# One weight load per page of instructions, a second bank for ranks, and a matmul block moved ahead of the last ranks

## The chip, the core and the metric

The kernel runs on one core of a Trainium2 chip. A core has five engines with a queue each: TensorE (PE, matrix products and transposes; PEld is its load of stationary weights), VectorE (DVE), ScalarE (ACT), GpSimd (POOL) and SyncE (SP), which here mostly starts DMA transfers. Every queue is served in order. Sixteen DMA engines move data between HBM and SBUF, and also bring the engines their instructions. PE writes only into PSUM, which has eight banks of 512 float32 per partition. The metric is the device time of one launch in microseconds; lower is better.

## The reference

Linear attention feeds a mixture of experts with one expert per token, and its output goes through a gated feed-forward layer.

```python
def phi(x):                                   # q, k: (2, 8, 576, 64), w_phi: (64, 128)
    proj = einsum('bhsd,df->bhsf', x, w_phi)
    proj = proj - max(abs(proj), axis=-1)
    return concatenate([exp(proj), exp(-proj)], axis=-1)
kv = einsum('bhsf,bhsd->bhfd', phi(k), v);  z = sum(phi(k), axis=2)
x  = (phi(q) @ kv) / (phi(q) @ z + 1e-6)      # as 1152 tokens of 512
e  = argmax(x @ w_gate);  g = softmax(x @ w_gate)[e]      # 8 experts
pos = number of earlier tokens with the same expert       # the token's rank
y  = g * (relu(x @ w1[e]) @ w2[e]) if pos < capacity else 0
out = (silu(y @ w_gate2) * (y @ w_val)) @ w_out           # 512 -> 1536 -> 512
```

## The kernel before

The 1152 tokens are nine tiles of 128. A first loop over tiles makes the k side (features, then the sums kv and z). A second loop over tiles, `for t in range(NT)` at line 664, makes the q side. It is a pipeline written out by hand: while tile t is projected and its exponentials are made, `q_num` (line 443) multiplies tile t-1 with kv in two halves of heads, `q_norm` divides tile t-2, `q_first` chooses its expert, and `q_rank` and `q_place` (lines 501 and 509) find the rank of each token of tile t-3 among those of its expert. After the loop the last tiles run out of the pipeline (lines 889 to 926).

`bank[6]` and `bank[7]` take the numerators of even tiles, `bank[2]` and `bank[3]` those of odd tiles. `sm` is another name for `bank[7]`, and all ranks are written there, into columns beyond the numerators. The second half of heads of an even tile therefore goes into the bank from which `q_place` has just to read the ranks of an earlier even tile, and PE holds that step back until VectorE has read them.

The tokens of a chosen expert are gathered by index (`gather`, GpSimd), transposed by PE (`transpose_x`), and go through the expert's two weight matrices in eight blocks. `h_mm(f)` is a block of the first matrix (eight matmul passes over 288 tokens), `y_mm(f)` the same block of the second. The expert with most tokens in the first tiles is the first item. Its weights, `raw[0]` to `raw[3]`, come in eight halves of 512 KB each: `h_mm(0)` and `h_mm(1)` read the first half of `raw[0]`, `h_mm(4)` and `h_mm(5)` the first of `raw[2]`. A second and a third item follow, then the feed-forward layer, whose weights arrive as `m2w` and are unpacked by ScalarE and VectorE beside the items.

`Paced` (line 79) counts the instructions that PE is given, and at every 256 of them, a page, lets transfers begin behind that step. Transfers in its list `waiting` come first; what is left of a page's budget, in KB, goes to the list `spare`, where the eight halves are put at tile 4. The budget is `FULL` = 800, and for tile 6 `MUCH` = 2048. `T.more(n)` starts n spare transfers at once, with no PE step to wait for.

Of the kernel before, what the change touches and what calls it, by code (L numbers as in the profile page):

```python
# [14 lines left out]
ALU = mybir.AluOpType  # L15
# [12 lines left out]
NT = N // P  # L28
E = 8
# [5 lines left out]
T0 = 2  # L35
# [9 lines left out]

MID = [(0, 0), (0, 1), (1, 0), (1, 1), (6, 0), (6, 1), (2, 0), (2, 1), (3, 0), (3, 1), (7, 0), (7, 1)]

PAGE, FIRST, ROOM, FULL, MUCH = 256, 193, 1060, 800, 2048

BESIDE = {  # L50
    0: {3: (("conv",),), 4: (("conv",),), 5: (("conv",),), 6: (("conv",),), 7: (("conv",),), 8: (("conv",),)},
# [18 lines left out]
RANK = [320] * (NT - 1) + [352]  # L70
# [8 lines left out]
class Paced:  # L79

    def __init__(self, engine):
        self.engine, self.count, self.at, self.waiting, self.spare, self.full = engine, 2, FIRST, [], iter(()), FULL

    def matmul(self, out, lhsT, rhs, **kw):
        return self.step(self.engine.matmul(out, lhsT=lhsT, rhs=rhs, **kw), 4 if lhsT.dtype == F32 else 2)  # L85
# [11 lines left out]
    def begin(self, x):  # L97

        used = 0
        while self.waiting and used + self.waiting[0][0] <= ROOM:  # L100
            size, load = self.waiting.pop(0)
            load(x)
            used += size
        while not self.waiting and used < self.full and self.count > FIRST + PAGE:
            size, load = next(self.spare, (self.full, None))
            if load is not None and used + size > self.full:
                self.spare = chain([(size, load)], self.spare)
                break
            if load is not None:
                load(x)  # L110
            used += size
# [13 lines left out]
def build(tc, qT, kT, v, wblk, wg, wexp, m2w, cap, cst, ids, out):  # L125
    nc = tc.nc
    ctx = ExitStack()
    V, A, G, T = nc.vector, nc.scalar, nc.gpsimd, Paced(nc.tensor)

    with ctx, tc.manual_schedule():  # L130
# [13 lines left out]
        capf = p0.tile([P, 1], F32, name="capf")  # L144
        sc = p0.tile([P, 4, 2, 12], F32, name="scan")
        est = p0.tile([P, 4, E], F32, name="est")
# [12 lines left out]
        ohsum = p0.tile([P, E], BF16, name="ohsum")  # L159
# [12 lines left out]
        bank = [pair[:, 0:512], pair[:, 512:1024], *(psm.tile([P, 512], F32, name=f"bank{j}") for j in range(2, 8))]  # L172
        xt, sm = bank[6:8]
# [6 lines left out]
        onebf = warm[:, 0:P]  # L180
# [13 lines left out]
        def behind(x, i):  # L194

            if i is not None:
                tc.add_manual_dep(x.ins, i.ins.name, mybir.DependencyInfo(mybir.DependencyClass.Sync, mybir.DependencyReason.DATA),
                                  reason="a load begins behind this step")
# [92 lines left out]
        def load_half(e, c, a, step=None):  # L291

            cols = slice(a * 1024, a * 1024 + 1024)
            behind(nc.sync.dma_start(out=raw[c][:, cols], in_=wexp[ds(e, 1), c].rearrange("a p f -> p (a f)")[:, cols]), step)
# [33 lines left out]
        if True:  # L328
# [4 lines left out]
            st = {}  # L333
# [38 lines left out]
            def later(size, load, *arg):  # L372
                T.later(size, lambda step: load(*arg, step))
# [5 lines left out]
            def g_turn(s, bk):  # L379

                for hp in range(NP):
                    T.transpose(bk[:, hp * P : hp * P + P], kvt[:, s, hp * P : hp * P + P], ident)
# [110 lines left out]
            def q_gate(t):  # L493
# [4 lines left out]
                A.activation(ex, lg, AF.Exp, scale=-1.0, bias=mx[:, 0:1], accum_out=mx[:, 2:3])  # L498
                A.activation(st[t + 1]["den"][:, H : H + 1], mx[:, 2:3], AF.Copy, bias=1e-9)

            def q_rank(t, *ahead):

                for c, w in ((RANK[t], ubf), *(((384, onebf),) if t in (T0 - 1, T0, NT - 1) else ())):
                    T.matmul(sm[:, c : c + E], lhsT=w, rhs=st[t]["oh"][2], start=True, stop=False)
                    for a in ahead:
                        T.matmul(sm[:, c : c + E], lhsT=onebf, rhs=st[a]["oh"][2], start=False, stop=False)
                    T.matmul(sm[:, c : c + E], lhsT=onebf, rhs=ohsum, start=False, stop=True)

            def q_place(t):

                mx, oh, ohb, lg = st[t]["oh"]
                V.tensor_tensor_reduce(oh, sm[:, RANK[t] : RANK[t] + E], ohb, 1.0, 0.0, ALU.mult, ALU.add, mx[:, 3:4])
                if t < NT - 2:
                    V.tensor_tensor(ohsum, ohsum, ohb, ALU.add)
                if t == T0 - 1:
                    V.tensor_copy(cnt0, sm[:, 384 : 384 + E])

            def q_put(t):

# [82 lines left out]
            def first_count():  # L602

                V.tensor_scalar(est[:, 0], cs[:, C_R8 : C_R8 + E], e0f[:, 1:2], None, ALU.is_equal)
                V.scalar_tensor_tensor(cnt0, sm[:, 384 : 384 + E], capf, est[:, 0], ALU.min, ALU.mult)

            def first_rest():

# [50 lines left out]
            cnt0 = pa.tile([P, E], F32, name="cnt0", bufs=1)  # L659
# [3 lines left out]
            for t in range(NT):  # L663
                if t + 3 < NT:
                    later(256, x_load, NT + t + 3)
                st[t + 1] = {}
                T.full = MUCH if t == T0 + 4 else FULL
                if t == 1:
                    g_turn(0, bank[2])
                    g_turn(1, bank[3])  # L670
                st[t]["pm"] = pb.tile([P, H, FP], F32, name="pm")
                maxima = less_max(bP, st[t]["pm"])
                norm = q_norm(t - 2) if t > 1 else iter(())
                late_ops = st[t - 3]["ops"] if t > 2 else iter(())
                next(maxima)
                next(maxima)
                next(late_ops, None)
                next(norm, None)
                next(late_ops, None)
                if t == 0:  # L680
                    k_sum(8, 9)
                else:
                    q_num(t - 1, 0)
                if t > 1:
                    q_phi(t, 0)
                if t > 2:
                    q_rank(t - 3)
                next(maxima)
                next(norm, None)
                if t > 2:  # L690
                    q_place(t - 3)
                if t == T0 + 3:
                    first_count()
                next(maxima)
                if t == 0:
                    k_take(1)
                    g_pack(1)
                    xrow = slot([96, 3, DM], F32, "xrow")
                    G.memset(xrow, 0.0)
                if t == 1:  # L700
                    g_copy(0, bank[2])
                    g_copy(1, bank[3])
                if t < 2:
                    q_phi(t, 0)
                step = q_exp(t, 0)
                if t == T0 + 5:
                    gather(0, (0, 1), step)
                elif t > 2:
                    q_put(t - 3)
                if t > 2:  # L710
                    x_store(t - 3, st[t - 2]["den"][:, H : H + 1])
                next(norm, None)
                if t:
                    q_num(t - 1, 1)
                if t == 1:
                    g_cols(1, bank[2])
                if t > 1:
                    ops = st[t - 2]["ops"] = q_first(t - 2)
                    choice = first_expert() if t == 4 else iter(())
                    for _ in range(3):  # L720
                        next(ops)
                        next(choice, None)
                    next(choice, None)
                    q_gate(t - 2)
                if t + 1 < NT:
                    T.until(lambda: NT + t + 1 in xraw)
                    project(xraw.pop(NT + t + 1), bP)
                q_phi(t, 1)
                step = q_exp(t, 1)
                if t == T0 + 5:  # L730
                    gather(0, (2,), step)
                    q_put(t - 3)
                if t == 4:
                    xch = slot([P, 4, 96, 3], F32, "xch")
                    raw = [slot([P, 2048], F32, f"raw{j}") for j in range(NC1)]
                    e = expert_of(0)
                    halves = [(512, lambda step, n=n: load_half(e, n // 2, n % 2, step)) for n in range(8)]
                    T.spare = chain(halves, T.spare)
                if t == T0 + 3:
                    load_list(0)  # L740
# [9 lines left out]
        def h_mm(f):  # L750
            c, r = f // 2, f % 2
            hp = bank[4 + f % 2][:, 0:WIN]
            for k in range(4):
                T.matmul(hp, lhsT=raw[c][:, k * 256 + r * P : k * 256 + r * P + P], rhs=xch[:, k].rearrange("p a b -> p (a b)"),
                         start=(k == 0), stop=(k == 3))
            A.activation(hh[f % 2], hp, AF.Relu)
# [129 lines left out]
        t = NT - 1  # L886
        def finish(ops):
            for _ in ops:
                pass
# [27 lines left out]
        h_mm(0)  # L917
        q_gate(t)
        finish(ops)
        q_rank(t - 1)  # L920
        q_rank(t, t - 1)
        for i in (t - 1, t):
# [3 lines left out]
        last = st[t + 1]["den"][:, H : H + 1]  # L926
        V.reciprocal(last, last)
        x_store(t, last)
        T.more(1)
        h_mm(1)  # L930
        y_mm(0)
        h_mm(2)
        y_mm(1)
# [3 lines left out]
        e = expert_of(1)  # L937
# [229 lines left out]
```

## Time and profile before

| | us |
|---|---|
| median of 3 runs (298.84 to 300.84) | 299.86 |
| the profiled execution | 297.08 |
| its span | 295.2 |
| PE busy in it | 280.4 (95%) |
| DVE, ACT, POOL busy in it | 193.8, 132.0, 41.4 |

The span runs from the first instruction to the last of the profiled execution. The times in the rows further down are microseconds from the span's start. A row of a timeline gives start, duration, engine, line, operation, what it writes and reads, and how many equal instructions in a row it stands for; in brackets is how long the engine stood idle before it, and what released it. Busy times of engines overlap. Only the idle time of an engine that the others wait for costs anything.

### The profile page before, as it was taken

How to read it: one execution, taken by the hardware profiler on the slowest of the kernel's cores; microseconds unless marked ns; L12 is line 12 of the kernel's file. 1: busy time of each engine (PE TensorE's matmuls, PEld its weight loads, DVE VectorE, ACT ScalarE, POOL GpSimd, SP SyncE). 2: the span in 40 equal slices, each digit the busy share in tenths (PEclk: the TensorE clock that was granted, in tenths of full speed). 3: DMA queues.
4: the chain of work that ended last, by engine and by line, in shares of the span. 5: the costliest groups of instructions: out<-in, count | busy, mean ns of one | idle time of the engine just before them, and what ended most of it. 6: DMA issues, size and time to landing. Idle time of an engine off the chain costs nothing. (4 is left out here: it accounts for less than half of the span.)

```text
span 295.2 us, 7725 instructions
## 1 busy us (share of the span) xinstructions
PE 280.4 (95%) x3195; PEld 243.3 (82%) x3195; DVE 193.8 (66%) x402; ACT 132.0 (45%) x255; POOL 41.4 (14%) x65
## 2 busy tenths in 40 slices
PE   7999999989979999999999999999999999999990
PEld 5899988877867777877775999999999899999970
DVE  1996885999948386799954788879876433223320
ACT  2877554767663242546456643553423322211210
POOL 3001030352654220006000000000010040000011
PEclk9999999999979999999999999999999999999998
DMA  6577654557973499999599205000416020000002
GB/s 210 180 233 205 194 183 156 168 203 210 321 260 116 126 322 381 417 405 359 194 394 363 91 2 143 0 2 0 142 52 271 2 109 0 0 2 1 2 2 75
DMA packets 18238, 47.96 MB, mean 162 GB/s; under 512 B 4353, under 2 KB 5542, under 8 KB 15632
## 3 DMA queue, kind: packets, MB, share of 16 engines
q1 hardware_dynamic: 16064, 44.39, 42.8%
q0 software_dynamic: 1264, 2.57, 2.6%
q8 instruction: 27, 0.44, 0.6%
q10 hardware_dynamic: 864, 0.39, 0.5%
q14 instruction: 19, 0.16, 0.2%
HBM read 41.06 MB, written 6.87 MB: 162 GB/s over the span
## 5 line engine op out<-in xcount | busy, mean ns | idle before, releaser
L85 PE MATMUL bank<-yh,m2h 128*128 128x384 f32 (+1 forms) x192 | 35.3, 305 | 0.0
L85 PE MATMUL bank<-yh,m2l 128*128 128x384 f32 (+1 forms) x192 | 35.2, 305 | 0.0
L85 PE MATMUL bank<-yl,m2h 128*128 128x384 f32 (+1 forms) x192 | 35.2, 305 | 0.0
L85 PE MATMUL bank<-xch,raw 128*128 128x288 f32 x128 | 33.7, 407 | 0.0
L85 PEld LDWEIGHTS bank<-yh,m2h 128*128 128x128 f32 x192 | 30.4, 188 | 2.5 <-issue 0.8
L995 ACT ACTIVATE th<-bank 128x384 fp32r<-128x384 f32 (+1 forms) x24 | 10.3, 431 | 43.2 <-DVE bank L994 43.2
L85 PEld LDWEIGHTS bank<-xch,raw 128*128 128x128 f32 x128 | 24.2, 190 | 6.6
L85 PEld LDWEIGHTS bank<-yh,m2l 128*128 128x128 f32 x192 | 29.6, 189 | 0.0
L85 PEld LDWEIGHTS bank<-yl,m2h 128*128 128x128 f32 x192 | 29.5, 189 | 0.0
L992 DVE TENSOR_TENSOR sg<-bank,sg 128x384 f32<-128x384 f32 (+1 forms) x24 | 11.6, 482 | 24.4 <-ACT sg L991 24.4
L85 PE MATMUL bank<-yk,phq 128*64 128x73 f32 x576 | 23.6, 235 | 2.5 <-issue 0.9
L85 PEld LDWEIGHTS bank<-yk,phq 128*64 128x64 f32 x576 | 20.8, 141 | 4.0 <-issue 1.4
L347 DVE TENSOR_REDUCE m<-bank 128x4 f32<-128x512 f32 x26 | 17.8, 686 | 8.4 <-PE bank L85 8.3
L283 DVE TENSOR_TENSOR m2l<-m2x,m2h 128x1024 fp32r<-128x1024 f32 x18 | 21.3, 1222 | 2.8 <-ACT m2h L282 2.7
L438 ACT ACTIVATE phq<-pair 128x512 f32<-128x512 f32 x36 | 19.5, 592 | 7.7 <-PE pair L88 7.6
L85 PE MATMUL bank<-vau,ph 128*64 128x65 f32 x640 | 21.9, 224 | 0.7 <-ACT ph L406 0.6
L85 PEld LDWEIGHTS bank<-vau,ph 128*64 128x64 f32 x640 | 20.1, 137 | 2.8 <-ACT ph L406 1.9
L991 ACT ACTIVATE sg<-bank 128x384 f32<-128x384 f32 (+1 forms) x24 | 10.3, 431 | 22.7 <-PE bank L85 22.7
L232 DVE SCALAR_TENSOR_TENSOR m2x<-es_mid,m2x 128x1024 uint32<-128x1024 uint32 x12 | 14.7, 1226 | 8.5 <-ACT es_mid L229 7.3
L996 DVE TENSOR_TENSOR tl<-bank,th 128x384 fp32r<-128x384 f32 (+1 forms) x24 | 11.6, 483 | 12.7 <-ACT th L995 12.7
L85 PE MATMUL bank<-m2h,th 128*128 128x512 f32 x48 | 19.1, 398 | 0.0
L85 PE MATMUL bank<-m2h,tl 128*128 128x512 f32 x48 | 19.1, 397 | 0.0
(159 smaller groups left out, 494.8 us busy)
## 6 DMA issues: line engine op xcount, KB each, us to landing
raw<-wexp SPq DMA_DIRECT2D x8, 1024.0 KB, 7.5
r<-m2w SPq DMA_DIRECT2D x8, 1024.0 KB, 8.0
r<-m2w SPq DMA_DIRECT2D x24, 256.0 KB, 4.0
raw<-wexp SPq DMA_DIRECT2D x8, 512.0 KB, 5.0
r_mid<-m2w SPq DMA_DIRECT2D x4, 1024.0 KB, 9.5
vau<-v SPq DMA_DIRECT2D x10, 260.0 KB, 3.6
qkr<-kT SPq DMA_DIRECT2D x9, 256.0 KB, 3.3
qkr<-qT SPq DMA_DIRECT2D x9, 256.0 KB, 2.8
```

The costliest lines, as they stand in the source:

```text
L85: return self.step(self.engine.matmul(out, lhsT=lhsT, rhs=rhs, **kw), 4 if lhsT.dtype == F32 else 2)
L232: V.scalar_tensor_tensor(w, es.bitcast(U32), 3, w, ALU.logical_shift_left, ALU.bitwise_or)
L283: V.tensor_tensor(m2l[j][:, sl], x[:, sl], m2h[j][:, sl], ALU.subtract)
L347: V.tensor_reduce(m[:, gs], pv, AX.X, ALU.max, apply_absolute_value=True)
L438: x = A.activation(st[t]["phq"][:, s, :, gs], bF[:, :, gs], AF.Exp, scale=1.0 - 2 * s)
L991: A.activation(s, pg, AF.Sigmoid)
L992: V.tensor_tensor(s, pg, s, ALU.mult)
L995: A.activation(th[f % 3][:, n], pv, AF.Copy)
L996: V.tensor_tensor(tl[f % 3][:, n], pv, th[f % 3][:, n], ALU.subtract)
```

## The change

The page budget stays at 800 KB throughout, so that one half (512 KB) begins per page and never four; the rest is started by `T.more(4)` behind the store of the last tile, where one half was started before. The ranks of tiles 0, 2, 4 and 6 go to `bank[3]`, the others stay in `bank[7]`. `h_mm(1)` stands ahead of the ranks of tiles 7 and 8, and no longer behind them and all that is made of them.

```diff
-PAGE, FIRST, ROOM, FULL, MUCH = 256, 193, 1060, 800, 2048
+PAGE, FIRST, ROOM, FULL = 256, 193, 1060, 800
...
-        while not self.waiting and used < self.full and self.count > FIRST + PAGE:
-            size, load = next(self.spare, (self.full, None))
-            if load is not None and used + size > self.full:
+        while not self.waiting and used < FULL and self.count > FIRST + PAGE:
+            size, load = next(self.spare, (FULL, None))
+            if load is not None and used + size > FULL:
...
+            ranks = [bank[3] if t % 2 == 0 and t < NT - 1 else sm for t in range(NT)]
+
             def q_rank(t, *ahead):
                 for c, w in ((RANK[t], ubf), *(((384, onebf),) if t in (T0 - 1, T0, NT - 1) else ())):
-                    T.matmul(sm[:, c : c + E], lhsT=w, rhs=st[t]["oh"][2], start=True, stop=False)
+                    r = ranks[t][:, c : c + E]
+                    T.matmul(r, lhsT=w, rhs=st[t]["oh"][2], start=True, stop=False)
...
-                V.tensor_tensor_reduce(oh, sm[:, RANK[t] : RANK[t] + E], ohb, 1.0, 0.0, ALU.mult, ALU.add, mx[:, 3:4])
+                V.tensor_tensor_reduce(oh, ranks[t][:, RANK[t] : RANK[t] + E], ohb, 1.0, 0.0, ALU.mult, ALU.add, mx[:, 3:4])
...
-                T.full = MUCH if t == T0 + 4 else FULL
...
         q_gate(t)
         finish(ops)
+        h_mm(1)
         q_rank(t - 1)
         q_rank(t, t - 1)
...
         x_store(t, last)
-        T.more(1)
-        h_mm(1)
+        T.more(4)
         y_mm(0)
```

How this moves instructions is seen at three places. The first is the queue of SP where the halves of the first item's weights begin (`raw_1304` to `raw_1307` are `raw[0]` to `raw[3]`, `xd<-yk` the stores of finished tiles). Lines with - stand there in the kernel before, with + in the changed one.

```order
 L294 DMA raw_1304<-wexp 128x1024
+L473 DMA xd<-yk 128x512
 L294 ISA
 L294 DMA raw_1305<-wexp 128x1024
+L473 DMA xd<-yk 128x512
 L294 ISA
 L294 DMA raw_1305<-wexp 128x1024
+L473 DMA xd<-yk 128x512 x3
 L294 ISA
 L294 DMA raw_1306<-wexp 128x1024
-L473 DMA xd<-yk 128x512
```

Two stores now stand between the second, third and fourth half, and all three last stores ahead of the other four halves, which follow each other.

The second place is PE in the second loop, tile 7: the ranks of tile 4 and then the second half of heads of tile 6 (`yk,phq`).

```order
 L85 LDWEIGHTS ubf_88
-L85 MATMUL bank7_102<-ohb_1514,ubf_88 128x8
+L85 MATMUL bank3_98<-ohb_1514,ubf_88 128x8
 L85 LDWEIGHTS warm_103
-L85 MATMUL bank7_102<-ohsum_87,warm_103 128x8
+L85 MATMUL bank3_98<-ohsum_87,warm_103 128x8
 L85 MATMUL bank7_102<-yk_92,phq_1481 64x73 x16
```

The ranks leave the bank into which the next sixteen matmuls write. The same holds for the ranks of tiles 0, 2 and 6.

The third place is PE where the pipeline runs out: the first item's block 0 (`xch,raw_1304` into `bank_99`), block 1 (into `bank_100`) and the ranks of tile 7.

```order
 L85 MATMUL bank_102<-yk,phq 64x73 x16
 L85 MATMUL bank_99<-xch,raw_1304 128x288 x4
+L85 MATMUL bank_100<-xch,raw_1304 128x288 x4
 L85 LDWEIGHTS ubf
 L85 MATMUL bank_102<-ohb,ubf 128x8
```

Block 1 moves ahead of the ranks; with the ranks, all that VectorE, GpSimd, ScalarE and SP make of them comes behind it.

## Rows read from the trace of the kernel before

**Rows 1.** The page, busy time and share of the span by engine.

```profile
PE 280.4 (95%) x3195; PEld 243.3 (82%) x3195; DVE 193.8 (66%) x402; ACT 132.0 (45%) x255; POOL 41.4 (14%) x65
```

**Rows 2.** Windows: length, busy time (instructions) by engine, granted clock, DMA share, GB/s.

```profile
71.40:80.90 9.50, 8.80 (x223) 7.71 (x220) 8.95 (x35) 6.62 (x17) 5.71 (x8) 1.00 0.95 298
84.00:87.70 3.70, 3.68 (x40) 3.12 (x40) 0.14 (x2) 2.40 (x6) 1.99 (x5) 0.54 0.54 202
92.70:153.00 60.30, 60.30 (x265) 47.10 (x263) 45.39 (x67) 25.59 (x38) 11.01 (x11) 1.00 0.85 314
```

**Rows 3.** Timeline of PE from tile 7 of the second loop to `y_mm(0)`.

```profile
74.00 1.25 PE L85 MATMUL bank<-yk,phq 128*64 128x73 f32 x32 [0.40 <-DVE mx L512]
...
81.85 0.60 PE L85 MATMUL bank<-yk,phq 128*64 128x73 f32 x11 [0.89 <-issue]
...
82.64 0.52 PE L88 MATMUL bank<-cs,xrow 96*128 96x96 f32 x4
84.02 0.80 PE L88 MATMUL bank<-cs,xrow 96*128 96x96 f32 x4 [0.86 <-DMA xrow<-xd,li]
...
85.62 2.15 PE L85 MATMUL bank<-yk,phq 128*64 128x73 f32 x32
87.71 2.21 PE L85 MATMUL bank<-xch,raw 128*128 128x288 f32 x8
...
90.51 0.17 PE L85 MATMUL bank<-ohb,ubf 128*128 128x8 bf16 x1 [0.57 <-DVE ohb L490]
...
90.67 2.19 PE L85 MATMUL bank<-xch,raw 128*128 128x288 f32 x8
92.69 1.13 PE L85 MATMUL pair<-hh,raw 128*128 128x288 f32 x4
```

**Rows 4.** Timeline of SP: where the first item's halves begin.

```profile
71.18 2.05 SPq L294 DMA_DIRECT2D raw<-wexp  x4
...
76.35 0.33 SPq L294 DMA_DIRECT2D raw<-wexp  x1
...
93.91 0.34 SPq L294 DMA_DIRECT2D raw<-wexp  x1
```

**Rows 5.** DMA queues, window 70.25 to 70.5: packets, MB, share of 16 engines.

```profile
q8 instruction: 1, 0.02, 23.0%
```

**Rows 6.** DMA queues, window 79.0 to 79.25: the next packet of that queue.

```profile
q8 instruction: 1, 0.02, 29.2%
```

**Rows 7.** DMA issues, window 66 to 92: count, median us from issue to landing.

```profile
xrow<-xd,li POOLq DMA_INDIRECT x3, 8.1
```

**Rows 8.** DMA issues, whole span: indirect stores at the kernel's end.

```profile
out<-room,gid POOLq DMA_INDIRECT x5, 2.9
```

**Rows 9.** Waits of PE up to 130 us: total us, times, longest.

```profile
PE bank L85 <- DVE cnt L605: 0.8, 1, 0.8
PE bank L85 <- DVE mx L512: 0.8, 2, 0.4
```

**Rows 10.** Timeline of DVE: tile 6's first maximum; tile 6's chosen expert.

```profile
66.78 0.69 DVE L347 TENSOR_REDUCE m<-bank 128x4 f32<-128x512 f32 x1 [0.21 <-PE bank L85]
...
81.31 0.22 DVE L490 TENSOR_SCALAR ohb<-oh,mx 128x8 bf16<-128x8 f32 x1
```

**Rows 11.** Timeline of ACT: last exponentials of the loop; a copy of transposed tokens.

```profile
81.36 1.06 ACT L438 ACTIVATE phq<-pair 128x512 f32<-128x512 f32 x2
...
85.73 0.69 ACT L321 ACTIVATE xch<-pair 128x384 f32<-128x384 f32 x1 [0.18 <-PE pair L88]
```

**Rows 12.** DMA issues, window 92 to 100: the eighth half alone.

```profile
raw<-wexp SPq DMA_DIRECT2D x1, 512.0 KB, 3.6
```

**Rows 13.** Tile `raw`, 60 to 180 us: landing times of all its loads.

```profile
DMA to landing us min/median/max: 3.6/6.7/13.6
```

**Rows 14.** Timeline of POOL: last gather of the second item.

```profile
104.54 0.95 POOL L309 DMA_INDIRECT xrow<-xd,li  x1 [0.31 <-PE bank L85]
```

**Rows 15.** Timeline of PE: transposes of the second item's tokens.

```profile
117.91 1.16 PE L88 MATMUL bank<-cs,xrow 96*128 96x96 f32 x12
```

More of the change, by code (lines that the diff above doesn't have):

```diff
@@ L81, in __init__ @@
     def __init__(self, engine):
-        self.engine, self.count, self.at, self.waiting, self.spare, self.full = engine, 2, FIRST, [], iter(()), FULL
+        self.engine, self.count, self.at, self.waiting, self.spare = engine, 2, FIRST, [], iter(())
     def matmul(self, out, lhsT, rhs, **kw):
@@ L499, in q_gate @@
                 A.activation(st[t + 1]["den"][:, H : H + 1], mx[:, 2:3], AF.Copy, bias=1e-9)
+            ranks = [bank[3] if t % 2 == 0 and t < NT - 1 else sm for t in range(NT)]
             def q_rank(t, *ahead):
                 for c, w in ((RANK[t], ubf), *(((384, onebf),) if t in (T0 - 1, T0, NT - 1) else ())):
-                    T.matmul(sm[:, c : c + E], lhsT=w, rhs=st[t]["oh"][2], start=True, stop=False)
+                    r = ranks[t][:, c : c + E]
+                    T.matmul(r, lhsT=w, rhs=st[t]["oh"][2], start=True, stop=False)
                     for a in ahead:
-                        T.matmul(sm[:, c : c + E], lhsT=onebf, rhs=st[a]["oh"][2], start=False, stop=False)
-                    T.matmul(sm[:, c : c + E], lhsT=onebf, rhs=ohsum, start=False, stop=True)
+                        T.matmul(r, lhsT=onebf, rhs=st[a]["oh"][2], start=False, stop=False)
+                    T.matmul(r, lhsT=onebf, rhs=ohsum, start=False, stop=True)
             def q_place(t):
                 mx, oh, ohb, lg = st[t]["oh"]
-                V.tensor_tensor_reduce(oh, sm[:, RANK[t] : RANK[t] + E], ohb, 1.0, 0.0, ALU.mult, ALU.add, mx[:, 3:4])
+                V.tensor_tensor_reduce(oh, ranks[t][:, RANK[t] : RANK[t] + E], ohb, 1.0, 0.0, ALU.mult, ALU.add, mx[:, 3:4])
                 if t < NT - 2:
@@ L515, in q_place @@
                 if t == T0 - 1:
-                    V.tensor_copy(cnt0, sm[:, 384 : 384 + E])
+                    V.tensor_copy(cnt0, ranks[t][:, 384 : 384 + E])
             def q_put(t):
@@ L604, in first_count @@
                 V.tensor_scalar(est[:, 0], cs[:, C_R8 : C_R8 + E], e0f[:, 1:2], None, ALU.is_equal)
-                V.scalar_tensor_tensor(cnt0, sm[:, 384 : 384 + E], capf, est[:, 0], ALU.min, ALU.mult)
+                V.scalar_tensor_tensor(cnt0, ranks[T0][:, 384 : 384 + E], capf, est[:, 0], ALU.min, ALU.mult)
             def first_rest():
@@ L736, in build @@
                     e = expert_of(0)
-                    halves = [(512, lambda step, n=n: load_half(e, n // 2, n % 2, step)) for n in range(8)]
+                    halves = [(512, lambda step, e=e, n=n: load_half(e, n // 2, n % 2, step)) for n in range(8)]
                     T.spare = chain(halves, T.spare)
```

## The prediction

> **What bounds the kernel now.** The page's table of engines comes first: PE is busy for 95% of the span [rows 1], so a gain can only come from PE's idle time, or from time in which PE is busy but slow. A table of windows then shows where these lie. From 92.7 to 153 us PE has no gap at all [rows 2]: what the change does before y_mm(0) is passed on in full, so long as nothing in that stretch becomes late. Between 71.4 and 80.9 PE is busy for 8.80 of 9.50 us, but VectorE for 8.95: there both take turns, and a wait of PE that disappears is not a gain of the same size. From 84.0 to 87.7 PE is busy without a break at a mean granted clock of 0.54, so nearly at the lower of its two levels, 1.2 GHz instead of 2.4 [rows 2].
>
> The timeline of PE up to y_mm(0) names the losses [rows 3]: 0.40 us for VectorE's reading of ranks at 74.00, 0.89 with no releaser but "issue" before 81.85, 0.86 for gathered tokens before 84.02, 0.57 for the last chosen expert before 90.51. Between the sixteen double matmuls at 80.9 and the second transposes at 84.02 PE did little, and after that the clock was low: four transposes took 0.80 instead of 0.52, the second half of heads 2.15 where 32 matmuls of the same form took 1.25 at 74.00.
>
> The last view is the queues. SP starts four halves in a row at 71.18 [rows 4], 2 MB, and the DMA engines are 95% busy from 71.4 to 80.9 [rows 2]. A packet of instructions arrives at 70.25 and the next only at 79.0 [rows 5, 6], 8.75 us later, though the page steps of PE, behind which the loads begin, are 5.2 us apart (71.18 and 76.35) [rows 4]. The stall follows less than 2 us after the start of the late packet. So I read "issue" as waiting for code, held up by the four halves. The gathers took 8.1 us to land in the same window [rows 7]; the indirect stores at the kernel's end, with the DMA otherwise idle, take 2.9 [rows 8].
>
> **The change part by part.** Ranks in the other bank: this removes three waits of PE, together 1.6 us [rows 9]; the fourth rank that moves, of tile 6, holds nobody up. The ends are 0 and 1.6. VectorE is the other half of the turn-taking and keeps its own work. Where it stood idle for PE, 0.21 us at tile 6's first maximum [rows 10], it can be served earlier by that much. I take 0.2 for each of the first two waits and 0.1 for the third: **0.5**, nearer to the lower end. No instruction is added, and the bank that now takes the ranks was read for the last time by VectorE before it is written.
>
> One half per page: SP issues the same eight halves of the same size, so the queue's own work is unchanged. With one half ahead of it instead of four, the packet should come near its time and the 0.89 go. Then VectorE binds: tile 6's chosen expert is ready at 81.31 + 0.22 = 81.53 [rows 10], 0.5 earlier by the ranks, so tile 6's ranks run at 81.1, and the transposes begin at 81.2 where they began at 82.64. The gathers are not reached by more than one half; I take them to land within 4.5 us (between 2.9 and 8.1 [rows 7, 8], nearer to the idle end since two halves and two stores in 10 us are about half of what the DMA moved there before), so the three groups of transposes follow each other, some 0.5 apart [rows 3], to 82.7. The third writes the bank that ScalarE's exponentials read until 81.36 + 1.06 = 82.42 [rows 11], 81.9 after the shift, which is in time. Since PE no longer stands idle for most of 3 us, I expect the clock to stay at its upper level; the second half of heads then takes 1.25 and ends at 83.9, not at 87.7. Now ScalarE is late next: three copies of 0.69 [rows 11] from 82.0 on end at 84.1. h_mm(0) begins at **84.2** instead of 87.71 [rows 3], 3.5 earlier (0.5 of it from the ranks).
>
> h_mm(1) ahead of the ranks: the chain from the second half of heads to the last chosen expert runs on VectorE beside both blocks. It took from 87.7 to 90.51 [rows 3], 2.8 us; from 83.9 it ends at 86.7, and the two blocks end at 84.2 + 2 x 2.0 = 88.2 (92.69 - 90.67 is one block). So PE no longer loses the 0.57; y_mm(0) begins at about 88.3 instead of 92.69 [rows 3], **4.4** earlier.
>
> What is queued behind it: the ranks themselves come at 88.3, not 90.6, so places, the last store, SP's loads and the work list move by 2.3 us only, 2.1 less than PE. SP begins the last four halves at 93.91 - 2.3 = 91.6 instead of one at 93.91 [rows 4]. A half alone landed 3.6 us after its issue [rows 12]: 95.2. PE asks for it at h_mm(4), five blocks after y_mm(0), 88.3 + 5 x 1.95 = 98.1. The cover is 2.9 us. Each later half follows by 1.7 us (512 KB at the 298 GB/s of the busy window [rows 2]), while PE asks for them 3, 4 and 7 blocks after the first, at 5.9 us and later. The three halves more are 1.5 MB, some 5 us of DMA, ahead of the second item's list. Its last gather began at 104.54 [rows 14] and its transposes at 117.91 [rows 15]; with 8.1 to land, 5.3 us of cover. If the gather is not earlier at all and PE is by 4.4, 0.9 is left. I cost that at nothing. After 153 nothing is touched.
>
> The sum: 297.1 us of the profiled execution less 4.4 is 292.7. The median of the runs shown is 2.8 higher, and a program of the same length should keep that: 299.9 - 4.4 = **295.5**.
>
> **The rivals.** A: the four halves were not the cause. The packet and the gathers are late for reasons of their own, the idle time before the transposes stays and the clock falls as before. Then only the ranks (0.5) and h_mm(1) (0.57) are left: 1.1 us, 298.8. For it speaks that the second item's gathers have no such burst before them and are not known to be quicker; against it the 8.75 us between two packets. The Trainium skill speaks for A in two places. "Runtime: NRT & Kernel Launch", section "Instruction fetch mechanics", says that an engine's sequencer fetches its next page on a DMA queue of its own while it runs the current one, and that crossing a page is mostly hidden. "DMA: Bandwidth & Descriptors", section "Queues, rings and completion order", says that each DMA engine takes turns between queues, packet by packet; by that a packet of code would wait for one packet of weights and not for four loads, and the sum would be the 1.1 of A. The trace shows the packet late in that very window, so it is not hidden here. I give A 0.18.
>
> B: part of it is given back. Either the clock still falls (the low stretch costs 0.28 in the second transposes, about as much in the third, and 0.90 in the heads, 1.5 in all), or the second item's gathers land 2 to 3 us later behind the additional 1.5 MB. The gain is 1.9 to 2.9, the time 297 to 298. Chance 0.13.
>
> C, the slower one: h_mm(4) waits for the fifth half. The loads of weights land after 6.7 us in the median and 13.6 at worst [rows 13]. From 91.6 the median comes at 98.3, even with the need at 98.1; beyond 6.5 us every microsecond is lost, and at 13.6 it is 7.1. A stall that long would also let the clock fall as it did at 84 (1.5). That leaves -4.4 + 7.1 + 1.5 = +4.2: 304.1. It decides from a landing of 11 us. Those slow loads lay in the saturated stretch behind several others, and the fifth half has only a store and its own like around it, so 0.05.
>
> The forecast has the remaining 0.64.
>
> **How the numbers follow.** About 1%, 3 us, is what a measurement of this kernel can tell from no change. The forecast is faster by 1.5%; it counts as faster but for a small share, B partly. Faster: 0.58 of the forecast and 0.05 of B, 0.63. Same: A, the rest of the forecast and of B, 0.32. Slower: C, 0.05. The low end has all of the ranks' 1.6 and no wait for ScalarE's copies, 1.1 + 0.4 more: 294.0. The high end takes in B and A: 298.9. What lies outside is C and the tails of the others.
>
> **What would show it.** In the changed profile: packets of instructions around 75 and 81 us, no "issue" before the end of the heads, gathers landing in 4 to 5 us, the granted clock 1.00 between 80 and 90, h_mm(0) and h_mm(1) back to back with no wait at the ranks, y_mm(0) near 88, no gap from there to 149. If the idle time around the transposes is there with one half per page, the reading of the burst is wrong; if it is gone and the span is not shorter by 4, a gap in the items must be named.

## The result and the profile after

The changed kernel takes **296.19 us** in the median (294.8 to 296.33, four runs) against 300.35 (298.84 to 301.21, four runs) for the kernel before beside it: a ratio of 0.9854, 95% interval 0.981 to 0.9898. Forecast were 295.5 us and 4.4 us of gain; measured are 4.2, and the interval of the ratio is 3.1 to 5.7 us of 300.35. The ratios, here and below, are not the quotients of the two medians, and leave out one slow run each of `e4` and `e7`. The two profiled executions lie closer together (297.08 and 294.80 us, spans 295.2 and 293.0): both were quicker than the median of their kernel, the one before by 3.3 us and the changed one by 1.4. In the traces y_mm(0) begins 2.73 us earlier, at 89.96 instead of 92.69 [rows 3].

The page of the changed kernel, the line that answers to [rows 1]:

```profile
PE 278.8 (95%) x3195; PEld 241.8 (83%) x3195; DVE 194.1 (66%) x402; ACT 132.0 (45%) x255; POOL 40.7 (14%) x65
```

PE has the same 3195 matmuls and is busy for 1.6 us less: those matmuls run quicker. Windows of the changed kernel (columns as in [rows 2]) show where:

```profile
71.40:80.90 9.50, 7.93 (x192) 6.86 (x192) 7.82 (x31) 5.90 (x15) 4.72 (x7) 1.00 0.64 183
...
84.00:87.70 3.70, 3.70 (x47) 3.06 (x46) 2.42 (x14) 3.39 (x9) 2.94 (x5) 1.00 0.63 214
92.00:153.00 61.00, 60.79 (x289) 47.29 (x287) 47.59 (x70) 26.56 (x40) 10.25 (x11) 1.00 0.94 350
```

From 84.0 to 87.7 the granted clock is 1.00 (2.4 GHz) where it was 0.54 [rows 2], and PE does 47 matmuls there instead of 40. DMA is busy for 64% of the first window instead of 95%. But PE does less in that first window than before: 192 matmuls instead of 223. The timeline of PE in the changed kernel shows why:

```profile
77.03 0.30 PE L85 MATMUL bank<-yk,phq 128*64 128x73 f32 x2 [0.24 <-issue]
77.76 1.07 PE L85 MATMUL bank<-yk,phq 128*64 128x73 f32 x26 [0.43 <-issue]
79.45 0.47 PE L88 MATMUL pair<-cs,pm 64*128 64x64 f32 x8 [0.63 <-DVE mx L488]
79.85 0.18 PE L85 MATMUL bank<-ohb,ubf 128*128 128x8 bf16 x1
...
83.27 0.17 PE L85 MATMUL bank<-ohb,ubf 128*128 128x8 bf16 x1 [0.37 <-DVE ohb L490]
...
83.37 0.85 PE L88 MATMUL bank<-cs,xrow 96*128 96x96 f32 x8
84.11 0.55 PE L88 MATMUL pair<-cs,xrow 96*128 96x96 f32 x4
84.59 1.25 PE L85 MATMUL bank<-yk,phq 128*64 128x73 f32 x32
85.77 4.15 PE L85 MATMUL bank<-xch,raw 128*128 128x288 f32 x16
...
89.96 1.22 PE L85 MATMUL pair<-hh,raw 128*128 128x288 f32 x4
```

There is a new hold-up at 77 us, which the kernel before did not have: PE's heads of tile 7 come in three pieces and the next step waits 0.63 for VectorE. The ranks that follow stand at 79.85, and stood at 78.28 in the trace of before: 1.57 us lost. From that row to y_mm(0) it took 14.41 us before and takes 10.11 now, 4.30 less. There is no "issue" inside the last heads, no wait for gathered tokens, heads at 1.25 instead of 2.15, both blocks as one row of 16 matmuls, and no wait at the last ranks. This is the forecast sequence, 1.6 us late.

The waits of PE from 45 to 95 us in the changed kernel (total, times, longest):

```profile
PE pair L88 <- DVE mx L488: 2.6, 4, 0.9
PE bank L85 <- issue: 0.7, 2, 0.4
```

The waits for ranks [rows 9] are gone, but waits for VectorE's line 488, two of 0.7 in all in the same stretch before, have become four of 2.6.

SP, and the landing of the gathers (window 66 to 92) in the changed kernel:

```profile
71.34 0.96 SPq L294 DMA_DIRECT2D raw<-wexp  x1
77.93 0.33 SPq L294 DMA_DIRECT2D raw<-wexp  x1
83.67 0.33 SPq L294 DMA_DIRECT2D raw<-wexp  x1
...
93.21 1.99 SPq L294 DMA_DIRECT2D raw<-wexp  x4
```

```profile
xrow<-xd,li POOLq DMA_INDIRECT x3, 4.8
```

One half begins per page, and the gathers land after 4.8 us instead of 8.1 [rows 7]. The packets of instructions start at 70.98, 76.00 and 83.15 in the changed kernel's record: the second one 5.0 us behind the first, where it was 8.8 in the kernel before (70.34 and 79.15).

### The profile page after: what moved, and what is told of

The parts are those of the page before. It is cut to its first block, busy times and chain, and to the rows that moved or that the text cites. A ratio compares the mean times of both kernels' runs of the same rounds, so it can differ in the third digit from the quotient of the medians.

```text
span 293.0 us, 7723 instructions
## 1 busy us (share of the span) xinstructions
PE 278.8 (95%) x3195; PEld 241.8 (83%) x3195; DVE 194.1 (66%) x402; ACT 132.0 (45%) x255; POOL 40.7 (14%) x65
## 5 line engine op out<-in xcount | busy, mean ns | idle before, releaser
L85 PEld LDWEIGHTS bank<-yk,phq 128*64 128x64 f32 x576 | 20.2, 136 | 2.1 <-issue 1.1
```

## Experiments

The theory, called BURST in the expectations, is that the four halves begun at once hold up the packet of instructions and the gathers, that PE then idles and the clock falls, and that h_mm(1) ahead covers what is uncovered after that. The rivals are that the bank of the ranks and the place of the block make the gain (ORDER in the expectations), that the parts act each for itself, and that the packet and the gathers are late in any case (rival A above: then all but the halves gives 1.1). The ratios are to the kernel before, run beside it on the same chip; its medians were 299.24, 296.91 and 297.61 us in the three groups of runs.

### The three parts alone, and all but the halves

The halves alone (`e1`): the budget and the rest of the loads, nothing else.

```diff
-                T.full = MUCH if t == T0 + 4 else FULL
...
-        T.more(1)
+        T.more(4)
```

> One half per page alone; ranks and the second block stay as before. Theory BURST (four halves begun in one page hold up PE's code and the gathers, PE then idles and its clock falls): faster by 2.5 to 3.5 us, ratio 0.988 to 0.992; no stall 'issue' in the numerators of the last tile, gathers landing in 4 to 5 us instead of 8, granted clock 1.00 from 80 to 90 us. Theory ORDER (the gain comes from the bank of the ranks and the place of the second block): within 0.5 us, ratio 0.998 to 1.002.

Measured: 298.85 us, 0.9983 (0.9957 to 1.001). The ranks alone (`e2`):

```diff
+            ranks = [bank[3] if t % 2 == 0 and t < NT - 1 else sm for t in range(NT)]
...
-                    T.matmul(sm[:, c : c + E], lhsT=w, rhs=st[t]["oh"][2], start=True, stop=False)
+                    T.matmul(ranks[t][:, c : c + E], lhsT=w, rhs=st[t]["oh"][2], start=True, stop=False)
```

> Ranks of even tiles in the other bank, alone. BURST: 0 to 0.5 us faster, ratio 0.998 to 1.000; the three waits for the ranks (1.6 us) vanish, and PE waits about as long for VectorE's maxima (line 488) one step later. ORDER: 1.0 to 1.6 us faster, ratio 0.995 to 0.997, no new wait.

Measured: 298.65 us, 0.9988 (0.9961 to 1.0015). The block alone (`e3`):

```diff
         finish(ops)
+        h_mm(1)
...
-        h_mm(1)
```

> The second block ahead of the last ranks, alone. BURST: about 0.6 us faster (the 0.57 us wait at the ranks), ratio 0.998; the clock still falls. ORDER: 2 us or more, ratio at most 0.994.

Measured: 298.58 us, 0.998 (0.9955 to 1.0006). The ranks and the block together, with the four halves kept as they were (`e4`; its edit is that of `e2` and `e3`):

> The changed kernel with the four halves in one page kept, so ranks and second block together. BURST: 1.1 us faster than before at most, ratio 0.996 to 0.998, with the stall, the late gathers and the low clock still there. ORDER: as the changed kernel, 4.2 us, ratio 0.985 to 0.988.

Measured: 298.34 us, 0.9963 (0.993 to 0.9996), 1.1 us of 299.24, with an interval of 0.1 to 2.1.

What follows: no part alone is told apart from nothing. For the halves BURST had forecast 2.5 to 3.5 us, and they gave 0.5. The trace of the halves alone shows what stood in the way. Timeline of PE there:

```profile
84.77 0.85 PE L88 MATMUL bank<-cs,xrow 96*128 96x96 f32 x8
85.57 0.55 PE L88 MATMUL pair<-cs,xrow 96*128 96x96 f32 x4
86.05 1.25 PE L85 MATMUL bank<-yk,phq 128*64 128x73 f32 x32
87.24 2.21 PE L85 MATMUL bank<-xch,raw 128*128 128x288 f32 x8
...
90.70 0.17 PE L85 MATMUL bank<-ohb,ubf 128*128 128x8 bf16 x1 [1.10 <-DVE ohb L490]
```

The transposes follow each other and the heads take 1.25, so the mechanism is there; but with only one block to cover VectorE, PE then waits 1.10 for the last chosen expert, where it waited 0.57 before [rows 3]. And the hold-up of 77 us is in this trace too, so the transposes begin late, at 84.77. With the burst kept, the same stretch reads (timeline of PE, `e4`):

```profile
84.22 0.52 PE L88 MATMUL bank<-cs,xrow 96*128 96x96 f32 x4
85.38 0.55 PE L88 MATMUL bank<-cs,xrow 96*128 96x96 f32 x4 [0.64 <-issue]
87.43 0.52 PE L88 MATMUL pair<-cs,xrow 96*128 96x96 f32 x4 [1.49 <-DMA xrow<-xd,li]
```

The third group waits 1.49 for its tokens, behind a gather that began at 79.79. But BURST had also forecast the stall in the heads and the low clock for `e4`, and this trace has neither: after the wait the heads take 1.25 and the two blocks 4.15.

### The parts in pairs, and the gathers set apart

On another chip: the changed kernel again (`e5`, no edit), the halves with the block (`e6`, the changed kernel with all ranks in `sm`), the halves with the ranks (`e7`, the changed kernel with `h_mm(1)` behind `T.more(4)`), and the changed kernel with its three gathers behind three different exponentials (`e8`), to see whether the hold-up of 77 us comes with two gathers close together:

```diff
-                    gather(0, (0, 1), step)
+                    gather(0, (0,), step)
+                if t == T0 + 6:
+                    gather(0, (2,), step)
...
-                    gather(0, (2,), step)
+                    gather(0, (1,), step)
```

> The changed kernel once more, beside the next three. Theory CHAIN (late gathers, then the wait for the last expert, lie behind each other on one chain, so taking one away alone uncovers the other): 3.0 to 4.4 us faster than before, ratio 0.985 to 0.990. Theory SUM (the parts only add up, 0.5 + 0.4 + 0.7 as measured alone): 1.5 us, ratio 0.994 to 0.996. In the profile the stall of PE ends 1.5 us after the start of the second gather again.

> One half per page and the second block ahead, ranks as before. CHAIN: 2.5 to 3.9 us faster, ratio 0.987 to 0.992, most of the whole change. SUM: 1.2 us, ratio 0.996.

> One half per page and the other bank for ranks, the second block behind the ranks as before. CHAIN: 0.5 to 1.2 us faster, ratio 0.996 to 0.998, and PE waits over 1 us for the last expert. SUM: 0.9 us, ratio 0.997; the wait for the last expert stays at 0.6.

> The changed kernel with the three gathers of the first item begun behind three different exponentials, about 2 us apart, instead of two in a row and one later. Theory PAIR (the stall of PE, VectorE and ScalarE near 77 us, whose end comes 1.5 us after the start of the second gather in five traces, is caused by that gather): the stall moves with the second gather, to about 79 to 80 us, or vanishes; 0 to 1 us faster than the changed kernel. Theory CODE (the stall is a page of instructions that comes late): the stall stays at the same place of PE's program, early in the numerators of tile 7.

Measured: `e5` 294.42 us, 0.9917 (0.9881 to 0.9953); `e6` 294.22, 0.9895 (0.9854 to 0.9935); `e7` 294.88, 0.9892 (0.9842 to 0.9941); `e8` 298.91, 1.006 (1.0026 to 1.0093).

The pairs with the halves in them give what the whole gives, within the intervals (3.1 us in `e6`, 3.2 in `e7`); which of the two small parts is needed beside the halves can't be told from these runs. Both theories miss: CHAIN had at most 1.2 us for `e7`, SUM 1.2 for `e6` and 0.9 for `e7`, and the wait for the last expert that both had in `e7` is not in its trace. The last experiment missed its forecast, 0 to 1 us faster than the changed kernel, and its aim: in no trace of this chip is there the hold-up, with gathers together or apart. It shows something else. Timeline of PE in the changed kernel again, and then with the gathers apart:

```profile
80.94 1.20 PE L88 MATMUL bank<-cs,xrow 96*128 96x96 f32 x8
83.32 0.52 PE L88 MATMUL pair<-cs,xrow 96*128 96x96 f32 x4 [1.19 <-DMA xrow<-xd,li]
83.77 1.25 PE L85 MATMUL bank<-yk,phq 128*64 128x73 f32 x32
```

```profile
85.57 0.87 PE L88 MATMUL pair<-cs,xrow 96*128 96x96 f32 x4 [2.87 <-DMA xrow<-xd,li]
86.38 2.21 PE L85 MATMUL bank<-yk,phq 128*64 128x73 f32 x32
```

Without the hold-up PE reaches the transposes at 80.94, 2.4 us sooner than in the first trace of the changed kernel, and the third group then waits 1.19 for a gather: the gathers land after 6.3 us here, not 4.8. A third gather begun later (80.97, not 76.81) makes that 2.87, the clock falls (heads 2.21), and the kernel is 4.5 us slower than `e5`. The waits for gathers are 2.1 us longer than in `e5` (2.87, and 0.45 for the second group, against 1.19), and y_mm(0) comes 3.7 later (92.84, not 89.14). So a late gather before this place can cost more than the wait for it, with no burst in it.

### The sum on one chip, and the gathers earlier

The last group, on the chip of the pairs, sets the whole (`e9`, no edit), the halves alone (`e10`) and the rest alone (`e11`) side by side, and adds a version that begins all three gathers one step of the loop earlier, ahead of the scatter of tile 3's list (`e12`):

```diff
-            def q_put(t):
+            def q_put(t, first=False):
...
+                if first:
+                    gather(0)
...
-                if t == T0 + 5:
-                    gather(0, (0, 1), step)
-                elif t > 2:
-                    q_put(t - 3)
+                if t > 2:
+                    q_put(t - 3, t == T0 + 4)
...
-                if t == T0 + 5:
-                    gather(0, (2,), step)
-                    q_put(t - 3)
```

> The changed kernel again, as the yardstick of this call. Both theories: ratio to before 0.985 to 0.992 (the two measurements so far were 0.985 and 0.992).

> One half per page alone, beside the yardstick on one chip. Theory GATHER (what the four halves cost is the late landing of the gathers, and with it at times the clock; the wait for the last expert lies behind it): 0.5 to 1.5 us faster than before, ratio 0.995 to 0.998; PE waits 1 us for the last expert. Theory HALVES (this part alone carries the gain): as the yardstick, 0.985 to 0.992.

> Four halves in one page, with the ranks and the second block as changed, beside the yardstick on one chip. GATHER: 1 to 1.5 us faster than before, ratio 0.995 to 0.997; the third transposes wait for the gather 1 us or more. If order alone made the gain (HALVES wrong the other way): as the yardstick.

> The changed kernel with all three gathers begun one step of the loop earlier, behind tile 3's place arithmetic, as soon as the list and the stores of tiles 0 to 2 have landed, about 1.2 us earlier for the first and 1 to 2 us for the third. GATHER: no wait for a gather before the transposes; 0.5 to 1.5 us faster than the yardstick. HALVES: no change against the yardstick, 0 to 0.3 us.

| | us | ratio (95%) | gain, us |
|---|---|---|---|
| `e10` halves alone | 295.52 | 0.9935 (0.9903 to 0.9967) | 1.9 |
| `e11` ranks and block | 296.61 | 0.9952 (0.9925 to 0.9979) | 1.4 |
| `e9` all | 293.69 | 0.988 (0.9831 to 0.993) | 3.6 |
| `e12` all, gathers earlier | 292.80 | 0.9838 (0.981 to 0.9866) | 4.8 |

The gains are (1 - ratio) x 297.61. GATHER had 0.5 to 1.5 us for `e10`, which gave 1.9, and 1 to 1.5 for `e11`, which gave 1.4; HALVES had `e10` like `e9`, and their intervals do overlap, but not more than 0.3 us by `e12` over `e9`, where the medians differ by 0.9. 1.9 + 1.4 = 3.3, and the whole has 3.6: on this chip the parts add up, and the halves are the larger one, though the two intervals overlap (1.0 to 2.9 and 0.6 to 2.2). Rival A had 1.1 for everything but the halves, and that is about what the rest gives (1.4 here, 1.1 in `e4`); what A denies, the gain by the halves, is there with an interval clear of 1.

The trace of the rest alone, with the burst, shows the stall again. Timeline of PE in `e11`:

```profile
79.16 0.92 PE L85 MATMUL bank<-yk,phq 128*64 128x73 f32 x21
80.89 0.60 PE L85 MATMUL bank<-yk,phq 128*64 128x73 f32 x11 [0.81 <-issue]
...
81.72 0.52 PE L88 MATMUL bank<-cs,xrow 96*128 96x96 f32 x4
83.53 0.57 PE L88 MATMUL bank<-cs,xrow 96*128 96x96 f32 x4 [1.29 <-DMA xrow<-xd,li]
84.70 0.87 PE L88 MATMUL pair<-cs,xrow 96*128 96x96 f32 x4 [0.60 <-DMA xrow<-xd,li]
85.50 2.21 PE L85 MATMUL bank<-yk,phq 128*64 128x73 f32 x32
87.65 5.66 PE L85 MATMUL bank<-xch,raw 128*128 128x288 f32 x16
```

It is the same instruction as in [rows 3], with 11 matmuls of those heads left, and 0.81 of "issue" instead of 0.89. Of the same kernel the DMA queues, window 78.5 to 78.75, with the late packet:

```profile
q8 instruction: 1, 0.02, 25.5%
```

By the records' starts this packet and the one before it stand at 78.64 and 69.84, 8.8 us apart, and the stall ends 2.25 us after the start of the later one. In `e9`, which differs in the halves alone, the second packet falls into the window 75.75 to 76, 4.7 us after the first (71.27):

```profile
q8 instruction: 1, 0.02, 32.0%
```

Timelines of PE in `e9` and in `e12`:

```profile
81.68 0.85 PE L88 MATMUL bank<-cs,xrow 96*128 96x96 f32 x8
83.40 0.52 PE L88 MATMUL pair<-cs,xrow 96*128 96x96 f32 x4 [0.88 <-DMA xrow<-xd,li]
83.85 1.25 PE L85 MATMUL bank<-yk,phq 128*64 128x73 f32 x32
85.03 4.15 PE L85 MATMUL bank<-xch,raw 128*128 128x288 f32 x16
89.22 1.22 PE L85 MATMUL pair<-hh,raw 128*128 128x288 f32 x4
```

```profile
81.89 0.85 PE L88 MATMUL bank<-cs,xrow 96*128 96x96 f32 x8
82.69 0.55 PE L88 MATMUL pair<-cs,xrow 96*128 96x96 f32 x4
83.17 1.25 PE L85 MATMUL bank<-yk,phq 128*64 128x73 f32 x32
84.35 4.15 PE L85 MATMUL bank<-xch,raw 128*128 128x288 f32 x16
88.54 1.22 PE L85 MATMUL pair<-hh,raw 128*128 128x288 f32 x4
...
131.32 2.21 PE L85 MATMUL bank<-xch,raw 128*128 128x288 f32 x8 [0.77 <-DMA raw<-wexp]
```

With the gathers earlier the wait of 0.88 is gone, and y_mm(0) comes at 88.54, close to the forecast 88.3. `e12` is the quickest of all, though its interval and that of `e9` overlap. Part comes back later: PE now waits 0.77 for the second item's weights.

## Why the prediction was right, and where its terms were off

**The cause.** That the burst holds up the packet of instructions is shown. The gap between the two packets is 8.4 to 8.8 us in the five traces with the burst (the kernel before, `e2`, `e3`, `e4`, `e11`) and 4.1 to 5.6 in the nine without. The place in PE's program says the same. A page of 256 instructions is about 128 matmuls with their weight loads here. In the nine traces the later packet starts 0.1 to 0.8 us after the matmul that stands 128 ahead of the stall's place, in the five 3.2 to 4.3 us after it. The stall at the 11 remaining matmuls is in two of the five and in none of the nine. It ends 2.70 us (the kernel before) and 2.25 us (`e11`) after the late packet's start; that PE waits there for this packet is read from place and time, and no row names it. In `e2` to `e4` PE came later to that place, behind the hold-up of 77 us, and the late packet (80.1 to 81.0) was there in time. The Trainium skill says in "Runtime: NRT & Kernel Launch", section "Instruction fetch mechanics", that crossing a page is mostly hidden: the nine traces agree, the burst does not. By the Trainium skill, "DMA: Bandwidth & Descriptors", section "Queues, rings and completion order", a packet of code should wait for one packet of weights at most. It is 3 to 4 us later under the burst, more than a whole load of 512 KB takes there (1.7 us at the 298 GB/s of [rows 2]), so here the measurement decides.

The DMA queues show that the gathers stood still as well. Window 76 to 78, the queue of the loads (q1) and that of the gathers (q0) in the kernel before:

```profile
q1 hardware_dynamic: 202, 0.75, 99.6%
q0 software_dynamic: 16, 0.00, 0.6%
```

The gathers in the same window of the changed kernel:

```profile
q0 software_dynamic: 63, 0.20, 49.8%
```

In both, two gathers had begun before the window or early in it (74.37 and 75.66, 74.95 and 76.25). In the kernel before the loads had the DMA engines to themselves. What in the engines gives the loads the way, no trace shows.

**The clock.** Right in its first trace: 1.00 from 84.0 to 87.7, heads at 1.25, the two blocks in a row at 4.15, where the sum had 2 x 2.0. It is not sure, however. Of the traces with the halves apart that wait 0.9 to 1.2 for a gather, `e5` and `e9` keep the clock, `e6` does not (heads 2.10, blocks 4.89), nor does `e7`, which waits twice (1.03 and 0.91, heads 2.22). With the burst it falls before or in the first block in three of five traces, and stays in `e3` and `e4`. The record has the mean granted clock of each execution too, though not where it fell. On the chip of `e5` to `e12` it is either 0.979 to 0.987 or 0.990 to 0.996. In the lower group are 28 of 45 executions of the kernel before, 11 of 12 of `e11`, all 12 of `e8`, 7 of 18 of the changed kernel (`e5`, `e9`) and none of 6 of `e12`. Within each group the changed kernel is still the quicker one: medians are 293.70 against 296.06 us in the upper group and 295.94 against 298.23 in the lower one beside `e5`, 293.05 against 296.92 and 295.76 against 298.05 beside `e9`. The sum had the clock always low before and never after; it falls in fewer executions now, and most of the gain on that chip is there without it, as far as groups of 2 to 18 executions tell.

**The gathers.** This term was sized too small. 4.5 us were forecast, with about half of the DMA traffic; the three traces of the changed kernel show 4.8, 6.3 and 5.7, and the first has 183 of the 298 GB/s. That goes unseen in the first, which comes late to the transposes, and costs 1.19 and 0.88 in the others. ScalarE's copies, named as late next, were not: `e10` waits 0.46 for one, the changed kernel for none. What was late next was the third gather, as `e12` shows by taking it away.

**The ranks.** The waits [rows 9] went, and as many came back at line 488, as the turn-taking of PE and VectorE let one expect for most of them. The 0.5 can't be told from nothing: 0.12% (-0.15 to 0.39) in `e2`, 0.4 us.

**The block.** Right: no wait at the last ranks in the changed kernel, where the halves alone wait 1.10 and 0.91. The step names 0.57 as its worth, but beside the halves it is worth what they uncover.

**Later stages.** Right but for a small term. The last four halves began at 93.21, not 91.6, as PE came later, and no block waited for them: rival C did not come about. From y_mm(0) to the end of the span it took 202.5 us before and takes 203.0 now, 202.8 in `e5`, 203.2 in `e9` and 203.5 in `e12`; in `e1` and `e10`, which have the same four loads in a row but reach y_mm(0) later, 202.4 and 202.6. So 0.3 to 1.0 us is given back in these traces. Coming earlier is not all of it: `e6` reaches y_mm(0) at 90.80, like `e10` (90.85), and takes 203.6, with a wait of 0.62 for the second item's weights. DMA is busy for 94% of 92 to 153 us in the changed kernel, and the new waits of PE are for transfers: 0.2 for tokens in its first trace, 0.3 and 0.77 for weights in `e9` and `e12`. This is a part of rival B, at a smaller size. That the DMA engines bind there was argued from these rows and not tried.

**The size.** 4.2 us in the first runs, 2.5 and 3.6 in the two repetitions on the chip of `e5` to `e12`, whose kernel before was quicker as well (296.91 and 297.61). The forecast of 4.4 is above all of these; the late third gather (0.9 to 1.2) and what is given back later (0.3 to 0.7) are of the size of the difference to the repetitions. That the first median came within 0.2 us of the forecast is in part luck: in its one trace y_mm(0) is 2.73 earlier and the span 2.2 shorter, with a hold-up of 1.57 that the sum did not have.

**Open.** The hold-up of 77 us. It is in the first trace of the changed kernel and in all four of the first group, with the burst and without, at different instructions of PE (tile 8's projection in `e1` and `e3`, tile 7's heads in the others), each time ending 1.50 to 1.54 us after the start of the second gather. It is absent in the kernel before and in all eight traces of the other chip, six of them with the same gathers. It comes with the burst and without, so it is not the late packet. `e8` was to settle it and couldn't.

## What to carry to other kernels

"issue" before an instruction in the middle of a row of equal matmuls is worth a look at the queue that brings instructions: if its packet starts just before, see what transfers were begun since the last one, and begin them one per page. An engine's wait that leads to a low clock costs more than itself, so of two late things before such a place the second must be moved as well; here the weights, and then the gathers (`e8` shows it clearly, `e12` within the noise). The same edit can be lost in the noise on one chip and be clear on another (the halves alone gave 0.5 us and 1.9), so the parts are tried alone, in pairs and beside the whole on one chip.

## What the runs showed that was not expected

- The gathers of the first item, 96 rows each, land after 3.7 to 7.0 us without the burst, in kernels that differ by little, and after 7.9 (`e11`) and 8.1 (the kernel before) with it; the profile gives no landing for `e2` to `e4`.
- A hold-up of PE, VectorE and ScalarE together of about 1 us, on some chips or in some executions only, as told above. In the first trace of the changed kernel VectorE and ScalarE stand idle beside PE:

```profile
77.89 0.69 DVE L347 TENSOR_REDUCE m<-bank 128x4 f32<-128x512 f32 x1 [1.35 <-PE pair L88]
```

```profile
78.07 1.09 ACT L438 ACTIVATE phq<-pair 128x512 f32<-128x512 f32 x2 [1.12 <-remote]
```

- After a wait of about the same length (0.94 in `e6`, 1.19 in `e5`) the granted clock fell to 0.50 in the first trace and stayed at 1.00 in the second, with the longer wait.
